# SwiGLU feed-forward on one core: the loads of the head issued in one line on SyncE's queue, the crossbar load of x rows 256 to 511 moved ahead of the first up weights, gate projection before up

## The chip, the cores and the metric

The kernel runs on one core of one Trainium2 chip. The metric is device time in microseconds (us) of that core. A profiled execution gives, besides, a span (first to last instruction) and a record of each instruction and each transfer; all start times below are counted from the start of that span.

## What is computed

The input x has 2048 rows of 640 numbers, the weights w_gate and w_up are 640 by 1536, and w_down is 1536 by 640, all bf16:

```python
def reference(x, w_gate, w_up, w_down):
    g = _silu(x @ w_gate)
    u = x @ w_up
    return (g * u) @ w_down
```

## The kernel before, in words

All three products run on TensorE. The 640 inner rows make 5 slices of 128 (KD, index kd), the 1536 hidden columns 12 slices (KF, index fc), and the 2048 rows of x four blocks of 512 (index sb). Gate and up are computed transposed: a weight slice of 128x128 is the stationary operand, and x transposed (xT, 128 partitions by kd by row) streams past it. So `proj` (line 193) makes five matmuls per output tile, one for each kd, and accumulates them in PSUM. `gate` (line 208) lets ScalarE take SiLU of the gate tile (L212) and VectorE multiply it with the up tile (L213) into aT. After the 12 slices of a block, the down projection multiplies aT with wd_sb (L270 and L299), and ScalarE copies and SyncE and ScalarE store the output. The last four rows of x are left to VectorE (`row_dots`, L148), which works them out beside TensorE.

**The head** is the first block's start, before all weights are there. x rows 0 to 255 come as two plain loads of 128 rows (x_sb, L86) and are transposed by TensorE (L186) and copied to xT by ScalarE and VectorE (L191). Rows 256 to 511 come by a transposing load through the DMA crossbar (`turn_x`, L110), straight into xT. Of the weights, the first chunk is 256 columns (fc 0 and 1), of gate and of up, 320 KB each; it is cut at kd = 2 (K_CUT) into a part of 128 KB and one of 192 KB.

In `head` (line 217) the order of TensorE's work is written out and fixed by `keep_order`: 18 filling matmuls on ones (L177), 10 transposes of x (L186), 2 more filling matmuls, then 14 matmuls of gate for fc 0 and 1 on x rows 0 to 255 (L237, the list `early`: kd 0 and 1 in halves of 128 columns, kd 2 to 4 in 256 columns). Then, in the kernel before, come up on rows 0 to 255 for fc 0 and 1 (10 matmuls of 256 columns), and then for each fc gate and up on rows 256 to 511 (20 matmuls of 256 columns). From fc = 2 on, every matmul of gate and up has 512 columns.

The loads are issued on two queues. SyncE (SPq) issues x rows 0 to 127, gate kd 0 to 1, up kd 2 to 4, the crossbar load, and after them the later weight chunks (L83), w_down (L126) and the rest. ScalarE (ACTq) issues x rows 128 to 255, gate kd 2 to 4 and up kd 0 to 1, then loads its SiLU table (L122). SyncE's issues keep their written order too (`keep_order` at the end). The four PSUM buffers with the tag `gu` hold the two gate and two up tiles of fc 0 and 1 at the same time.

Of the kernel before, what the change touches and what calls it, by code (L numbers as in the profile page):

```python
# [10 lines left out]
def _body(  # L11
# [8 lines left out]
    nc = tc.nc  # L20
# [12 lines left out]
    KD = D // P  # L33
    KF = F // P
    S_BLK = 512
# [8 lines left out]
    K_CUT = 2  # L44
    ROW_J = 0
    W_CHUNKS = [(0, 2), (2, 4), (4, 8), (8, 12)]
# [12 lines left out]
    wg_sb = consts.tile([P, KD, F], bf16)  # L59
    wu_sb = consts.tile([P, KD, F], bf16)  # L60
# [14 lines left out]
    wg_v = w_gate.rearrange("(kd p) f -> p kd f", p=P)  # L75
    wu_v = w_up.rearrange("(kd p) f -> p kd f", p=P)
    wd_v = w_down.rearrange("(kf p) d -> p kf d", p=P)

    def wslice(a, b):
        return slice(a * P, b * P)  # L80

    def load_w(eng, dst, src, a, b):
        eng.dma_start(out=dst[:, :, wslice(a, b)], in_=src[:, :, wslice(a, b)])  # L83

    def load_x(eng, c0, c1):
        eng.dma_start(out=x_sb[:, c0:c1, :], in_=x_v[:, c0:c1, :])  # L86
# [11 lines left out]
    def keep_order(engine):  # L98

        traced = [i for i in nc.cur_bb.bb.instructions if i.engine == engine]  # L100
        for a, b in zip(traced, traced[1:]):
            issue_order(a, b)
# [5 lines left out]
    def turn_x(c0, c1):  # L108
        s_sl = slice(c0 * P, c1 * P)
        nc.sync.dma_start_transpose(out=xT[:, :, s_sl], in_=xt_v[s_sl])  # L110

    load_x(nc.sync, 0, 1)
    load_x(nc.scalar, 1, 2)
    f_sl = wslice(*W_CHUNKS[0])
    for dst, src, first, second in (
        (wg_sb, wg_v, nc.sync, nc.scalar),
        (wu_sb, wu_v, nc.scalar, nc.sync),
    ):
        for eng, k_sl in ((first, slice(0, K_CUT)), (second, slice(K_CUT, KD))):
            eng.dma_start(out=dst[:, k_sl, f_sl], in_=src[:, k_sl, f_sl])  # L120
    turn_x(PE_X, SUB)
    nc.scalar.activation(silu_first[:], ones[:, 0:1], ACT.Silu)  # L122
    for a, b in W_CHUNKS[1:]:
        load_w(nc.sync, wg_sb, wg_v, a, b)
# [5 lines left out]
    def turn_w(dst, src):  # L130
# [7 lines left out]
        out=x_row[:],  # L138
        in_=x2[S - T : S, :].rearrange("t d -> (t d)").partition_broadcast(P),
# [35 lines left out]
    def warm(n):  # L175
        for _ in range(n):
            nc.tensor.matmul(  # L177
                pw[:, 0:P], lhsT=ones[:], rhs=ones[:], start=True, stop=True
            )

    def transpose_chunk(c, parts):
        c_sl = slice(c * P, (c + 1) * P)
        for copy, tag, k0, k1 in parts:
            pt = psum.tile([P, k1 - k0, P], bf16, tag=tag, name="pt")
            for kd in range(k0, k1):
                nc.tensor.transpose(  # L186
                    out=pt[:, kd - k0, :],
                    in_=x_sb[:, c, kd * P : (kd + 1) * P],
                    identity=ident[:],
                )  # L190
            copy(out=xT[:, k0:k1, c_sl], in_=pt[:])  # L191

    def proj(ps, w_sb, fc, sb, c0, c1):
        for kd in range(KD):
            nc.tensor.matmul(  # L195
                ps[:, c0:c1],
                lhsT=w_sb[:, kd, fc * P : (fc + 1) * P],
                rhs=xT[:, kd, sb * S_BLK + c0 : sb * S_BLK + c1],
                start=(kd == 0),
                stop=(kd == KD - 1),  # L200
            )

    def gu_tiles():
        pg = psum.tile([P, S_BLK], f32, tag="gu", name="pg", bufs=4)
        pu = psum.tile([P, S_BLK], f32, tag="gu", name="pu", bufs=4)
        return pg, pu

    def gate(pg, pu, sb, fc, n_s):

        s0 = sb * S_BLK  # L210
        sg = work.tile([P, S_BLK], f32, name="sg")
        nc.scalar.activation(sg[:, 0:n_s], pg[:, 0:n_s], ACT.Silu)  # L212
        nc.vector.tensor_tensor(  # L213
            out=aT[:, fc, s0 : s0 + n_s], in0=sg[:, 0:n_s], in1=pu[:, 0:n_s], op=ALU.mult
        )

    def head():

        dve, act = nc.vector.tensor_copy, nc.scalar.copy
        split = [(act, "po_a", 0, 2), (dve, "po_b", 2, KD)]
        late = PE_X * P
        (pg0, pu0), (pg1, pu1) = gu_tiles(), gu_tiles()
        warm(N_WARM)
        transpose_chunk(0, split)
        transpose_chunk(1, split)
        warm(N_GAP)  # L230
        early = [(kd, c * P, (c + 1) * P) for c in range(PE_X) for kd in range(K_CUT)]
        early += [(kd, 0, late) for kd in range(K_CUT, KD)]
        for kd, c0, c1 in early:
            for fc, pg in ((0, pg0), (1, pg1)):


                nc.tensor.matmul(  # L237
                    pg[:, c0:c1],
                    lhsT=wg_sb[:, kd, wslice(fc, fc + 1)],
                    rhs=xT[:, kd, c0:c1],  # L240
                    start=(kd == 0 and c0 == 0),
                    stop=(kd == KD - 1),
                )
        proj(pu0, wu_sb, 0, 0, 0, late)
        proj(pu1, wu_sb, 1, 0, 0, late)
        for fc, pg, pu in ((0, pg0, pu0), (1, pg1, pu1)):
            proj(pg, wg_sb, fc, 0, late, S_BLK)
            proj(pu, wu_sb, fc, 0, late, S_BLK)
            gate(pg, pu, 0, fc, S_BLK)
        keep_order(mybir.EngineType.PE)  # L250
        keep_order(mybir.EngineType.Activation)

    head()
    for sb in range(NSB):
        n_s = S_BLK if sb < NSB - 1 else S_BLK - T
        for fc in range(KF):
            if sb == 0 and fc < 2:
                continue
            pg, pu = gu_tiles()
# [22 lines left out]
        for q in range(P // Q):  # L282
            nc.scalar.dma_start(
                out=out2[
                    sb * S_BLK : sb * S_BLK + n_t, DA + q * Q : DA + (q + 1) * Q
                ].rearrange("(i r) c -> r i c", r=Q),
                in_=ot_q[q * Q : (q + 1) * Q, :].rearrange("r (i c) -> r i c", c=Q),
            )

        for j in range(SUB):  # L290
# [5 lines left out]
            for c0, c1, tag in cols:  # L296
# [10 lines left out]
                if c1 < D:  # L307
                    nc.scalar.copy(ot[:], po[:])  # L308
                    eng = nc.sync
                else:  # L310
                    nc.vector.tensor_copy(out=ot[:], in_=po[:])  # L311
                    eng = nc.scalar
# [81 lines left out]
def kernel(tc, *args):  # L394
    _body(tc, *args)
    tc.close()
    tc.compile()
    _trim(tc.nc)
# [30 lines left out]
```

## Time and profile before

| what | us |
|---|---|
| median of 3 runs (lowest, highest) | 163.66 (163.46, 163.86) |
| span of the profiled execution | 162.17 |
| median less span: what lies around the span, if that execution was a median one | 1.49 |
| TensorE busy, share of the span | 159.8, 99% |
| VectorE busy | 110.9 |
| ScalarE busy | 42.7 |
| first matmul of fc = 2 (the head's work is behind it) | 9.11 |

The profiled execution has no time of its own besides its span, so the median of the runs stands in for it. A matmul's record holds its whole passage through the array, and the next starts before it ends; so the pace is read from start to start. Of the span, 99% on the chain of waits that ended last is TensorE; the granted clock in the rows is full throughout. A transfer's row gives the queue that issued it, its size, and the time from issue to landing; issue start plus that time is when the waiting engine may go on.

### The profile page before, as it was taken

The numbers are of one execution on the slowest core, as the hardware profiler recorded it, in microseconds if no ns is written. First come the engines' busy times: TensorE is split into PE (matmuls) and PEld (weight loads), VectorE is DVE, ScalarE is ACT, GpSimd is POOL, SyncE is SP. The second block draws the span as 40 slices with busy tenths as digits, with TensorE's granted clock in tenths as the row PEclk, the third lists the DMA queues.
The fourth block names the chain that finished last, engine by engine and source line by source line (L and its number), as shares of the span: only waits on it lengthen the run. The fifth ranks groups of instructions, "written<-read, shape, count | busy, mean of one in ns | idle before, by whom it ended". The sixth has DMA issues, their size and how long they took to land.

```text
span 162.2 us, 2118 instructions
## 1 busy us (share of the span) xinstructions
PE 159.8 (99%) x798; PEld 77.9 (48%) x798; DVE 110.9 (68%) x249; ACT 42.7 (26%) x74; POOL 0.6 (0%) x6
## 2 busy tenths in 40 slices
PE   9999999999999999999999999999999999999995
PEld 8854444444444444444444444444444444445454
DVE  2042233599469999979919999979964999993000
ACT  5132222112222222221222322221214222222121
POOL 1000000000000000000000000000000000000000
PEclk9999999999999999999999999999999999999999
DMA  7999999994179992003110000000320000000312
GB/s 208 258 339 348 362 218 249 219 234 94 34 185 178 224 195 61 4 0 34 65 65 0 0 4 2 0 0 2 63 69 32 0 0 0 0 0 4 50 39 73
DMA packets 42441, 15.86 MB, mean 98 GB/s; under 512 B 33216, under 2 KB 42304, under 8 KB 42432
## 3 DMA queue, kind: packets, MB, share of 16 engines
q1 hardware_dynamic: 33536, 14.72, 37.7%
q10 hardware_dynamic: 8896, 1.02, 4.1%
q8 instruction: 6, 0.10, 0.2%
q14 instruction: 3, 0.02, 0.1%
HBM read 6.88 MB, written 2.62 MB: 59 GB/s over the span
## 4 chain that ended last, share of the span: by engine, by line
PE 99%; DVE 0%; issue 0%
PE pu L195 32%; PE pg L195 31%; PE po_a L299 26%; PE po_t L270 6%; PE pw L177 1%; PE pg L237 1%; PE pt L186 1%; DVE ot_b L311 0%; DVE ones L106 0%
## 5 line engine op out<-in xcount | busy, mean ns | idle before, releaser
L195 PE MATMUL pu<-xT,wu_sb 128*128 128x512 bf16 (+2 forms) x250 | 59.8, 370 | 0.0
L195 PE MATMUL pg<-xT,wg_sb 128*128 128x512 bf16 (+2 forms) x240 | 58.5, 374 | 0.0
L213 DVE TENSOR_TENSOR aT<-sg,pu 128x512 bf16<-128x512 f32 (+1 forms) x48 | 32.8, 683 | 32.8 <-PE pu L195 28.1
L212 ACT ACTIVATE sg<-pg 128x512 f32<-128x512 f32 (+1 forms) x48 | 28.6, 596 | 71.2 <-PE pg L195 68.1
L299 PE MATMUL po_a<-wd_sb,aT 128*128 128x512 bf16 (+2 forms) x216 | 42.8, 358 | 0.0
L148 DVE SCALAR_TENSOR_TENSOR prod<-wgT,x_row 128x640 f32<-128x640 bf16 x48 | 39.4, 821 | 1.1
L148 DVE SCALAR_TENSOR_TENSOR prod<-wuT,x_row 128x640 f32<-128x640 bf16 x48 | 39.4, 822 | 1.0
L195 PEld LDWEIGHTS <-wu_sb 128*128 128x128 bf16 x250 | 24.4, 98 | 27.6 <-DMA wu_sb<-in_w_up_dram 0.3
L195 PEld LDWEIGHTS <-wg_sb 128*128 128x128 bf16 x240 | 23.5, 98 | 26.9
L299 PEld LDWEIGHTS <-aT 128*128 128x128 bf16 x216 | 20.7, 98 | 21.6
L308 ACT CAST ot<-po_a 128x512 bf16<-128x512 f32 (+1 forms) x17 | 9.5, 560 | 32.0 <-PE po_a L299 20.8
L270 PE MATMUL po_t<-aT,wd_sb 128*128 128x512 bf16 (+1 forms) x48 | 10.4, 366 | 0.0
L270 PEld LDWEIGHTS <-wd_sb 128*128 128x128 bf16 x48 | 4.7, 98 | 5.1
L311 DVE CAST ot_b<-po_a 128x128 bf16<-128x128 f32 x1 | 0.3, 291 | 9.9 <-PE po_a L299 9.9
L279 ACT CAST ot_t<-po_t 128x512 bf16<-128x512 f32 (+1 forms) x4 | 2.2, 558 | 11.6 <-PE po_t L270 11.6
L148 DVE DVE_READ_ACCUMULATOR prod<-wuT,x_row 128x1 f32 x48 | 3.9, 82 | 0.0
L148 DVE DVE_READ_ACCUMULATOR prod<-wgT,x_row 128x1 f32 x48 | 3.9, 82 | 0.0
L281 DVE STREAM_TRANSPOSE ot_q<-ot_t 128x512 bf16<-128x512 bf16 (+1 forms) x4 | 2.7, 678 | 1.7 <-ACT ot_t L279 1.7
L177 PE MATMUL pw<-ones 128*128 128x128 bf16 x20 | 2.5, 313 | 0.4 <-DVE ones L106 0.4
L191 DVE COPY xT<-pt 128x384 bf16<-128x384 bf16 x2 | 0.7, 358 | 2.9 <-PE pt L186 2.9
L237 PE MATMUL pg<-xT,wg_sb 128*128 128x128 bf16 (+1 forms) x14 | 2.3, 360 | 0.0
L177 PEld LDWEIGHTS <-ones 128*128 128x128 bf16 x20 | 2.1, 148 | 0.4 <-DVE ones L106 0.4
(15 smaller groups left out, 7.6 us busy)
## 6 DMA issues: line engine op xcount, KB each, us to landing
wd_sb<-in_w_down_dram SPq DMA_DIRECT2D x1, 1920.0 KB, 14.5
out_dram<-ot SPq DMA_DIRECT2D x15, 128.0 KB, 1.7
wg_sb<-in_w_gate_dram SPq DMA_DIRECT2D x2, 640.0 KB, 7.7
wu_sb<-in_w_up_dram SPq DMA_DIRECT2D x2, 640.0 KB, 8.7
x_row<-in_x_dram SPq DMA_DIRECT2D x1, 640.0 KB, 4.7
out_dram<-ot_q ACTq DMA_DIRECT2D x12, 32.0 KB, 1.9
wg_sb<-in_w_gate_dram SPq DMA_DIRECT2D x1, 320.0 KB, 4.9
wu_sb<-in_w_up_dram SPq DMA_DIRECT2D x1, 320.0 KB, 5.4
```

Of the source, the lines that this page charges most:

```text
L148: nc.vector.scalar_tensor_tensor(out=prod[:], in0=wT[:, fc, :], scalar=1.0, in1=x_row[:, t, :], op0=ALU.mult, op1=ALU.mult, accum_out=acc[ ...
L177: nc.tensor.matmul(pw[:, 0:P], lhsT=ones[:], rhs=ones[:], start=True, stop=True)
L186: nc.tensor.transpose(out=pt[:, kd - k0, :], in_=x_sb[:, c, kd * P : (kd + 1) * P], identity=ident[:],)
L195: nc.tensor.matmul(ps[:, c0:c1], lhsT=w_sb[:, kd, fc * P : (fc + 1) * P], rhs=xT[:, kd, sb * S_BLK + c0 : sb * S_BLK + c1], start=(kd == 0 ...
L212: nc.scalar.activation(sg[:, 0:n_s], pg[:, 0:n_s], ACT.Silu)
L213: nc.vector.tensor_tensor(out=aT[:, fc, s0 : s0 + n_s], in0=sg[:, 0:n_s], in1=pu[:, 0:n_s], op=ALU.mult)
L237: nc.tensor.matmul(pg[:, c0:c1], lhsT=wg_sb[:, kd, wslice(fc, fc + 1)], rhs=xT[:, kd, c0:c1], start=(kd == 0 and c0 == 0), stop=(kd == KD ...
L270: nc.tensor.matmul(po_t[:], lhsT=wd_sb[:, kf, DA:D], rhs=aT[:, kf, sb * S_BLK : sb * S_BLK + n_t], start=(kf == 0), stop=(kf == KF - 1),)
L279: nc.scalar.copy(ot_t[:], po_t[:])
L281: nc.vector.transpose(out=ot_q[:], in_=ot_t[:])
L299: nc.tensor.matmul(po[:], lhsT=aT[:, kf, s0 : s0 + P], rhs=wd_sb[:, kf, c0:c1], start=(kf == 0), stop=(kf == KF - 1),)
L308: nc.scalar.copy(ot[:], po[:])
```

## The change

All six loads of the head (there were seven) are issued by SyncE, in the order x rows 0 to 127, x rows 128 to 255, gate kd 0 to 1, gate kd 2 to 4, the crossbar load of x rows 256 to 511, and then the first up chunk as one load of 320 KB. ScalarE issues none of them. On TensorE the 14 early gate matmuls stay; behind them now come gate on rows 256 to 511 for fc 0 and 1 (10 matmuls of 256 columns), and then for each fc up on all 512 rows (10 matmuls of 512 columns in all in place of 20 of 256).

```diff
     load_x(nc.sync, 0, 1)
-    load_x(nc.scalar, 1, 2)
+    load_x(nc.sync, 1, 2)
     f_sl = wslice(*W_CHUNKS[0])
-    for dst, src, first, second in (
-        (wg_sb, wg_v, nc.sync, nc.scalar),
-        (wu_sb, wu_v, nc.scalar, nc.sync),
-    ):
-        for eng, k_sl in ((first, slice(0, K_CUT)), (second, slice(K_CUT, KD))):
-            eng.dma_start(out=dst[:, k_sl, f_sl], in_=src[:, k_sl, f_sl])
+    for k_sl in (slice(0, K_CUT), slice(K_CUT, KD)):
+        nc.sync.dma_start(out=wg_sb[:, k_sl, f_sl], in_=wg_v[:, k_sl, f_sl])
     turn_x(PE_X, SUB)
+    load_w(nc.sync, wu_sb, wu_v, *W_CHUNKS[0])
     nc.scalar.activation(silu_first[:], ones[:, 0:1], ACT.Silu)
...
-        proj(pu0, wu_sb, 0, 0, 0, late)
-        proj(pu1, wu_sb, 1, 0, 0, late)
+        proj(pg0, wg_sb, 0, 0, late, S_BLK)
+        proj(pg1, wg_sb, 1, 0, late, S_BLK)
         for fc, pg, pu in ((0, pg0, pu0), (1, pg1, pu1)):
-            proj(pg, wg_sb, fc, 0, late, S_BLK)
-            proj(pu, wu_sb, fc, 0, late, S_BLK)
+            proj(pu, wu_sb, fc, 0, 0, S_BLK)
             gate(pg, pu, 0, fc, S_BLK)
```

## The prediction

> **What bounds the kernel now.** I read the page's busy times first (TensorE 159.8 of 162.2 us), then the chain of waits that ended last (99% TensorE, no transfer in it), then the timeline of the first 12 us, then the transfers. The change touches only the head, so its worth is the shift of one moment: the first matmul of fc = 2, at 9.11 in the timeline. From there on TensorE runs without a gap (five 512-column matmuls in 1.08 us, 9.11 to 10.19, again and again), so a shift of that moment should reach the end whole.
>
> The timeline's columns are start, length, engine and line. Start to start is the pace.
>
> ```profile
> 0.40 2.10 PE L177 MATMUL pw<-ones 128*128 128x128 bf16 x18 [0.40 <-DVE ones L106]
> ...
> 1.43 1.63 SPq L110 DMA_TRANSPOSE xT<-in_x_dram  x1
> ...
> 2.29 1.31 PE L186 MATMUL pt<-ident,x_sb 128*128 128x128 bf16 x10
> ...
> 3.61 2.34 PE L237 MATMUL pg<-xT,wg_sb 128*128 128x128 bf16 x14
> ...
> 5.80 1.01 PEld L195 LDWEIGHTS <-wu_sb 128*128 128x128 bf16 x10 [0.32 <-DMA wu_sb<-in_w_up_dram]
> 5.80 1.29 PE L195 MATMUL pu<-xT,wu_sb 128*128 128x256 bf16 x10
> ...
> 6.92 0.71 PE L195 MATMUL pg<-xT,wg_sb 128*128 128x256 bf16 x5
> ...
> 9.11 1.24 PE L195 MATMUL pg<-xT,wg_sb 128*128 128x512 bf16 x5
> ...
> 10.19 1.24 PE L195 MATMUL pu<-xT,wu_sb 128*128 128x512 bf16 x5
> ```
>
> See that TensorE is already back to back from 0.40: 18 filling matmuls take 1.89 us (0.105 each), and in the trace every 128-column matmul up to 4.36 starts 0.107 after the one before, and every 256-column one up to 5.53 takes 0.213. From 5.94 on a 256-column matmul takes 0.109 and a 512-column one 0.216. So TensorE runs at half pace until about 5.8, although the rows show the full granted clock, and the first 5.75 us of its work are bound by its own pace, not by a load. The only idle time is 0.05 us (5.75 to 5.80), where it waits for up weights.
>
> The head's transfers, from the list of transfers (last column: us from issue to landing):
>
> ```profile
> wg_sb<-in_w_gate_dram ACTq DMA_DIRECT2D x1, 192.0 KB, 3.6
> wu_sb<-in_w_up_dram SPq DMA_DIRECT2D x1, 192.0 KB, 4.7
> x_sb<-in_x_dram SPq DMA_DIRECT2D x1, 160.0 KB, 2.2
> x_sb<-in_x_dram ACTq DMA_DIRECT2D x1, 160.0 KB, 2.7
> wg_sb<-in_w_gate_dram SPq DMA_DIRECT2D x1, 128.0 KB, 2.8
> wu_sb<-in_w_up_dram ACTq DMA_DIRECT2D x1, 128.0 KB, 4.7
> ```
>
> The same list for issues between 1.4 and 3 us has the crossbar load:
>
> ```profile
> xT<-in_x_dram SPq DMA_TRANSPOSE x1, 5.4
> ```
>
> With the issue starts of the timeline the landings are: x rows 0 to 127 at 2.25, rows 128 to 255 at 2.85, gate kd 0 to 1 at 3.25, gate kd 2 to 4 at 4.20, up at 5.75, the crossbar load at 1.43 + 5.4 = 6.82. The head is balanced to within 0.1: up is there when gate is done (5.75), the crossbar load when up on 256 rows is done (6.9).
>
> **The change on TensorE.** Up to 5.75 nothing changes in work or order. After it, before: 30 matmuls of 256 columns, 30 x 0.109 = 3.27. After: 10 x 0.109 = 1.09 and 10 x 0.216 = 2.16, together 3.25. The change of pace costs 0.035 on one matmul either way (5.80 to 5.94). If no load is late, fc = 2 starts at 5.75 + 0.035 + 3.25 = 9.04 instead of 9.11: **-0.07 us**. ScalarE and VectorE: both SiLUs now start early, the first product (0.69) follows the first up tile at about 7.9, and the PSUM buffer that fc = 3 needs at about 11.2 is free near 7.7; nothing waits. ScalarE's table load, which began at 1.58 behind three issues of 0.41 to 0.51, starts sooner; the copy that it delayed is ahead of need anyway.
>
> **The change on the queue.** SP's issues take 0.40 to 0.47 and start 0.46 apart, so x rows 128 to 255 are issued at 0.46 (were at 0.12), gate at 0.92 and 1.38, the crossbar load at 1.85 (was 1.43) and, after its 1.63, up at 3.53. Needs and supplies:
>
> - x rows 128 to 255, needed at 2.83; before, landed at 2.85. Both x loads are ahead of all else now; the bytes that had moved by 2.2 were 320 KB, so about 2.6. Hidden.
> - Gate kd 2 to 4, needed at 4.36. Before, 640 KB had moved by 3.4, but shared with up; now the first 640 KB are just x and gate. Engines are up to 0.7 apart (completion packets of this load 3.14 to 3.84), so 3.8 for the last, plus 0.4 to land: 4.2. Bounds 3.9 and 4.5, price 0 to 0.15; I take 0.
> - The crossbar load, needed at 5.75 + 0.035. Three estimates. By bytes: 320 KB of up are no longer ahead of it; the next 320 KB load landed 1.16 behind it before (3.11 + 4.9 = 7.98), so 6.82 - 1.16 = 5.66. By issue: a crossbar load onto idle queues (issued at 44.88) had sent as many packets 2.75 after its issue; 1.85 + 2.75, plus 0.65 for landing as here, is 5.25. By the slowest engine, see below: 5.45. I take **5.45**, hidden by 0.3. Bounds: 5.25, and 1.85 + 5.4 = 7.25 if nothing is gained by going earlier.
> - Up, needed at 5.79 + 1.09 = 6.87. It stands behind the crossbar load as the later gate chunk did: 5.45 + 1.16 = **6.6**, hidden by 0.25. Bounds 6.4 and 8.4.
>
> The third estimate reads the transfer view from 4.5 to 5.5, 40 slices of 0.025 us:
>
> ```profile
> GB/s 338 246 297 348 287 246 297 246 277 225 236 236 225 195 164 195 164 164 102 143 123 92 51 92 31 0 20 20 20 10 20 20 20 143 174 154 205 123 133 174
> ```
>
> The rate falls to near nothing at 5.1 and comes back at 5.33. Crossbar packets of the fast engines hang there, and all are released together just after the slowest engine, done with up at 5.14, has begun its own. From its beginning to the end of all the packets it is 0.95 (5.1 to 6.05), then 0.7 to land. With the slowest engine done with gate at 3.8: 3.8 + 0.95 + 0.7 = 5.45.
>
> The later chunks keep their place: 1.28 MB lie ahead of them as before, and gate of fc 2 and 3 landed at 7.98 for a need at 9.11. If the covers above go, every us late at 5.79 or 6.87 is a us at the end.
>
> **Sum.** Span 162.17 - 0.07 = 162.10, plus the 1.49 around it, 163.59; I say **163.6** against the median of 163.66.
>
> **Rivals.**
>
> *The crossbar load stays the late one (slower).* The wait for up at 5.75 becomes one for xT, and up behind it is late too. For it: the load waits for the slowest of 16 engines, three loads of its kind further on show packets that hang 0.8 to 1.2, and it is issued 0.42 later. Against: 320 KB fewer ahead. It decides from a landing of 5.79 for xT or 6.87 for up. At 6.3, halfway to the upper bound from 5.45, fc = 2 starts at 6.3 + 3.25 = 9.55, and up (7.46 + 2.16 = 9.62) sets it: +0.5, **164.2**. At the upper bound it is 8.4 + 2.16 = 10.56, +1.45.
>
> *One queue starts its transfers a whole us apart (slower).* On SP's queue the first packets of its loads came at 1.02, 1.98, 3.05 and 4.10, while ScalarE's came between them. If that is one queue's own limit, gate kd 2 to 4 starts at 4, the crossbar load at 5.1, and lands 2.2 to 2.7 later, at 7.3 to 7.8; 3.25 more gives 10.6 to 11.0, **165.2 to 165.6**. Against it speak ScalarE's four stores at 112.5, alone on their queue, in slices of 0.06 us:
>
> ```profile
> GB/s 0 0 0 33 64 89 84 79 84 82 33 0 28 62 85 89 79 81 82 42 0 27 58 87 80 86 83 87 39 0 30 65 87 81 89 92 78 25 0 0
> ```
>
> They start 9 slices, 0.54 us, apart: one queue does one each half us, so the us in the head was two queues taking turns. [...]
>
> *The pace steps up earlier (faster).* In the one trace it steps at 5.8. If in other runs it steps at 4.3, the early gate ends at 4.36 + 6 x 0.109 = 5.0. Before, that gained nothing: up landed at 5.75, and 5.75 + 3.27 = 9.02. After, with the lower bounds (xT 5.25, up 6.4), fc = 2 starts at 6.4 + 2.16 = 8.56: -0.45, **163.2**. Against it: the spread of 163.46 to 163.86 gives no sign, and both loads must be at their best. [...]
>
> *The change doesn't do what it says.* The order on TensorE and SyncE is fixed by hand, so this would only mean that one load slips; it gives the forecast's time.
>
> **Chances.** Forecast 0.52 (with the last rival); crossbar load late 0.26; one queue a us apart 0.10; earlier step 0.12. A difference of 0.2%, 0.33 us, is about what a measurement of this kernel can tell from none. All of the first slower rival's and the second's chance counts as slower, so faster 0.12, same 0.52, slower 0.36. The range must leave out no more than 0.2: from 163.3 (part of the fast case) to 164.5 (most of the late crossbar load); the us-apart case lies beyond. The forecast's own range is 163.4 to 163.9.
>
> **What the profile of the changed kernel would show.** Right: 14 early gate matmuls ending near 5.75, gate of rows 256 to 511 at 5.8, up at 6.9, fc = 2 near 9.04; crossbar landing 3.6 after its issue at 1.85, up 3.1 after 3.53. Wrong: idle time of TensorE's weight loads put down to xT or wu_sb, first packets of SP's loads a us apart, x rows 128 to 255 landing past 2.85, or gate past 4.36, which would stretch the early gate.

## The result and the profile after

The changed kernel takes **164.87 us** (median of 4 runs, 164.81 to 165.12) beside 163.61 for the kernel before: ratio **1.0089**, 95% interval 1.0074 to 1.0105. A second measurement gave 164.78 beside 163.54 (1.0071, 1.0048 to 1.0095). The forecast was 163.6 with a range to 164.5; the change is slower. A ratio here is an estimate of its own from the same runs, not the quotient of the two medians beside it (1.0077 here), and for e3 it leaves out one slow run of 166.88, at a granted clock of 0.99.

The profiled execution has a span of 163.58 us, 1.41 more than before. The page's chain now has a transfer and SyncE's issues in it, where before it was TensorE alone:

```profile
PE 94%; DMA 3%; SPq 2%; issue 0%; DVE 0%
```

The timeline of the head (start, length, engine, line; in brackets idle time ahead and what ended it):

```profile
1.90 1.40 SPq L110 DMA_TRANSPOSE xT<-in_x_dram  x1
...
3.34 0.58 SPq L83 DMA_DIRECT2D wu_sb<-in_w_up_dram  x1
...
3.74 0.62 PE L234 MATMUL pg<-xT,wg_sb 128*128 128x128 bf16 x8
...
5.00 0.83 PE L234 MATMUL pg<-xT,wg_sb 128*128 128x256 bf16 x6 [0.64 <-DMA wg_sb<-in_w_gate_dram]
...
6.28 1.25 PE L192 MATMUL pg<-xT,wg_sb 128*128 128x256 bf16 x10 [0.45 <-DMA xT<-in_x_dram]
...
8.34 2.33 PE L192 MATMUL pu<-xT,wu_sb 128*128 128x512 bf16 x10 [0.81 <-DMA wu_sb<-in_w_up_dram]
...
10.51 1.24 PE L192 MATMUL pg<-xT,wg_sb 128*128 128x512 bf16 x5
```

See four starts of TensorE, each behind a load: gate kd 0 to 1 (3.74), gate kd 2 to 4 (5.00), the crossbar load (6.28), up (8.34). The gate of fc = 2 starts at 10.51 in place of 9.11, and these 1.40 us are the whole difference: span less start of fc = 2 is 153.07 us in the profiles of both kernels, and in all the experiments below to 0.01. So each run can be read by that one start.

The list of transfers of the changed kernel's head has the landings (last column: us from issue):

```profile
wu_sb<-in_w_up_dram SPq DMA_DIRECT2D x1, 320.0 KB, 4.9
...
wg_sb<-in_w_gate_dram SPq DMA_DIRECT2D x1, 192.0 KB, 3.6
wg_sb<-in_w_gate_dram SPq DMA_DIRECT2D x1, 128.0 KB, 2.8
xT<-in_x_dram SPq DMA_TRANSPOSE x1, 4.3
```

With the issue starts: gate kd 0 to 1 at 3.70, gate kd 2 to 4 at 4.96, the crossbar load at 6.24, up at 8.29.

A load's landing is the last of 16 completions, and the trace has each. Two things are seen there. First, gate kd 2 to 4: one completion at 3.79, then none for a whole us, then 15 from 4.79 to 4.96. The transfer view from 4 to 5 (slices of 0.025 us) shows why:

```profile
GB/s 256 256 266 287 276 307 287 297 297 184 184 154 102 82 61 41 20 20 20 20 20 21 20 20 10 20 20 20 20 92 205 225 143 287 297 276 276 307 287 287
```

From 4.25 the rate dies away to 20 GB/s, one packet of 512 bytes a slice, until 4.73: about what one engine moves alone, at 0.03 us a packet. Gate's completion packets (4 bytes each, 16 for this load) agree: 15 went by 3.91, the last at 4.55. Crossbar packets begun from 4.20 on hang, and end together between 4.73 and 4.77. I call the end of that stretch, 4.77, the **release**. Second, up: 15 completions from 7.26 to 7.36, and the last at 8.29. One engine is late by 0.93.

### The profile page after: what moved, and what is told of

It is laid out like the page before. It is cut to its first block, busy times and chain, and to the rows that moved or that the text cites. A ratio compares the mean times of both kernels' runs of the same rounds, so it can differ in the third digit from the quotient of the medians.

```text
span 163.6 us, 2097 instructions
## 1 busy us (share of the span) xinstructions
PE 159.2 (97%) x788; PEld 76.2 (47%) x788; DVE 110.9 (68%) x249; ACT 42.8 (26%) x74; POOL 0.6 (0%) x6
## 4 chain that ended last, share of the span: by engine, by line
PE 94%; DMA 3%; SPq 2%; issue 0%; DVE 0%
PE pu L192 32%; PE pg L192 30%; PE po_a L295 26%; PE po_t L266 6%; DMA wu_sb<-in_w_up_dram 3%; SPq L110 1%; SPq L116 1%; SPq L86 0%; DVE ot_b L307 0%
## 5 line engine op out<-in xcount | busy, mean ns | idle before, releaser
L192 PE MATMUL pu<-xT,wu_sb 128*128 128x512 bf16 (+1 forms) x240 | 59.4, 379 | 0.8 <-DMA wu_sb<-in_w_up_dram 0.8
L192 PEld LDWEIGHTS <-wu_sb 128*128 128x128 bf16 x240 | 23.4, 98 | 29.1 <-DMA wu_sb<-in_w_up_dram 1.1
L234 PE MATMUL pg<-xT,wg_sb 128*128 128x128 bf16 (+1 forms) x14 | 1.4, 243 | 0.8 <-DMA wg_sb<-in_w_gate_dram 0.6
```

Source lines behind the costliest of these rows:

```text
L192: nc.tensor.matmul(ps[:, c0:c1], lhsT=w_sb[:, kd, fc * P : (fc + 1) * P], rhs=xT[:, kd, sb * S_BLK + c0 : sb * S_BLK + c1], start=(kd == 0 ...
```

## The experiments

I started from theory A (the place of the crossbar load is the cost, by its release and by what stands behind it) and theory B (one queue in place of two is the cost).

### e1: one queue, up ahead of the crossbar load, TensorE's order as before

```diff
 (the kernel before)
     load_x(nc.sync, 0, 1)
-    load_x(nc.scalar, 1, 2)
+    load_x(nc.sync, 1, 2)
     f_sl = wslice(*W_CHUNKS[0])
-    for dst, src, first, second in (
-        (wg_sb, wg_v, nc.sync, nc.scalar),
-        (wu_sb, wu_v, nc.scalar, nc.sync),
-    ):
-        for eng, k_sl in ((first, slice(0, K_CUT)), (second, slice(K_CUT, KD))):
-            eng.dma_start(out=dst[:, k_sl, f_sl], in_=src[:, k_sl, f_sl])
+    for k_sl in (slice(0, K_CUT), slice(K_CUT, KD)):
+        nc.sync.dma_start(out=wg_sb[:, k_sl, f_sl], in_=wg_v[:, k_sl, f_sl])
+    load_w(nc.sync, wu_sb, wu_v, *W_CHUNKS[0])
     turn_x(PE_X, SUB)
```

> All loads on SyncE's queue as in the changed kernel, but the first up chunk ahead of the crossbar load, and TensorE's order as before. Theory A (the crossbar load's place is the cost: completions of the loads near it are held until its slowest engine has begun, and up stands behind it): gate kd 2 to 4 lands near 4.2, up near 5.7, the crossbar load near 6.8, fc = 2 starts near 9.1 to 9.3, time 163.6 to 163.8. Theory B (one queue in place of two is the cost: each load starts later): up lands past 7, fc = 2 past 10, time 164.5 or more.

Measured: 163.95 beside 163.40, ratio 1.0016 (1.0000 to 1.0031). Up landed at 5.90, the crossbar load at 7.07. Theory B's 164.5 is out; one queue by itself costs less than the whole change (the medians are 0.55 us apart, against 1.26 there). What it costs is seen in one row:

```profile
9.67 1.25 PE L192 MATMUL pg<-xT,wg_sb 128*128 128x512 bf16 x4 [0.22 <-DMA wg_sb<-in_w_gate_dram]
```

The gate chunk of fc 2 and 3, behind the crossbar load, has its median completion at 8.10 and its last at 9.63: again late engines in the load behind the crossbar load.

### e2: two queues, the crossbar load ahead of up, gate first

```diff
 (the changed kernel)
-    load_x(nc.sync, 1, 2)
+    load_x(nc.scalar, 1, 2)
-    for k_sl in (slice(0, K_CUT), slice(K_CUT, KD)):
-        nc.sync.dma_start(...)
+    for eng, k_sl in ((nc.sync, slice(0, K_CUT)), (nc.scalar, slice(K_CUT, KD))):
+        eng.dma_start(out=wg_sb[:, k_sl, f_sl], in_=wg_v[:, k_sl, f_sl])
```

> ScalarE issues x rows 128 to 255 and gate kd 2 to 4 again; on SyncE's queue x, gate kd 0 to 1, the crossbar load, then up; TensorE's order as in the changed kernel. Theory A: gate kd 0 to 1 is back at 3.25, but gate kd 2 to 4 still lands near 4.8, the crossbar load near 6.1 and up near 8.2; fc = 2 near 10.4, time 164.8. Theory B: gate kd 2 to 4 at 4.2, the crossbar load near 5.5, up near 6.6, time 163.6.

Measured: 164.43 beside 163.40, 1.0056 (1.0040 to 1.0072). The time is nearer to A's; the landings up to the crossbar load are nearer to B's (gate kd 2 to 4 at 4.34, the crossbar load at 5.49).

```profile
5.55 1.25 PE L192 MATMUL pg<-xT,wg_sb 128*128 128x256 bf16 x10
7.89 2.11 PE L192 MATMUL pu<-xT,wu_sb 128*128 128x512 bf16 x9 [1.09 <-DMA wu_sb<-in_w_up_dram]
9.84 1.24 PE L192 MATMUL pg<-xT,wg_sb 128*128 128x512 bf16 x5
```

Here the crossbar load did land at 5.49, where the forecast had put it (release 4.12), and gate on rows 256 to 511 followed the early gate without idle time. (The record of the first of the ten up matmuls, near 7.68, is missing.) It was no use: up came at 7.62 (median of its completions 6.96), where B had 6.6.

### e3: loads of the kernel before, gate first

```diff
 (the kernel before)
-        proj(pu0, wu_sb, 0, 0, 0, late)
-        proj(pu1, wu_sb, 1, 0, 0, late)
+        proj(pg0, wg_sb, 0, 0, late, S_BLK)
+        proj(pg1, wg_sb, 1, 0, late, S_BLK)
         for fc, pg, pu in ((0, pg0, pu0), (1, pg1, pu1)):
-            proj(pg, wg_sb, fc, 0, late, S_BLK)
-            proj(pu, wu_sb, fc, 0, late, S_BLK)
+            proj(pu, wu_sb, fc, 0, 0, S_BLK)
```

> TensorE's order of the changed kernel with the loads of the kernel before. The crossbar load should land at 6.8 and up at 5.75, so TensorE waits from the end of the early gate to 6.8 and then has 1.09 + 2.16 us of work: fc = 2 at 10.1, +0.95 on 9.11, time 164.6, by theory A and by theory B. If it is nearer to 163.6, the order on TensorE is no part of the cost.

Measured: 164.36 beside 163.40, 1.0046 (1.0025 to 1.0067); fc = 2 at 10.11, the expected 10.1. TensorE waits for xT:

```profile
6.87 1.25 PE L195 MATMUL pg<-xT,wg_sb 128*128 128x256 bf16 x10 [0.74 <-DMA xT<-in_x_dram]
8.17 2.10 PE L195 MATMUL pu<-xT,wu_sb 128*128 128x512 bf16 x9
10.11 1.24 PE L195 MATMUL pg<-xT,wg_sb 128*128 128x512 bf16 x5
```

Gate first makes x rows 256 to 511 the load that 3.25 us of work stand behind; with up first it is 2.2.

### e4: loads of the changed kernel, up first

```diff
 (the changed kernel)
-        proj(pg0, wg_sb, 0, 0, late, S_BLK)
-        proj(pg1, wg_sb, 1, 0, late, S_BLK)
+        proj(pu0, wu_sb, 0, 0, 0, late)
+        proj(pu1, wu_sb, 1, 0, 0, late)
         for fc, pg, pu in ((0, pg0, pu0), (1, pg1, pu1)):
-            proj(pu, wu_sb, fc, 0, 0, S_BLK)
+            proj(pg, wg_sb, fc, 0, late, S_BLK)
+            proj(pu, wu_sb, fc, 0, late, S_BLK)
```

> Loads of the changed kernel, TensorE's order of the kernel before: up on rows 0 to 255 ahead of gate on rows 256 to 511. If up lands at 8.3 as in the changed kernel, 30 matmuls of 0.109 follow it: fc = 2 at 11.6, time 166.0. If up lands at 7.3 (15 of its 16 completions came by 7.36 in the changed kernel, the last at 8.29), fc = 2 at 10.6, time 165.0.

Measured: 166.55 beside 163.40, 1.0174 (1.0122 to 1.0226).

```profile
8.13 1.27 PE L192 MATMUL pu<-xT,wu_sb 128*128 128x256 bf16 x10 [1.89 <-DMA wu_sb<-in_w_up_dram]
...
11.41 1.24 PE L192 MATMUL pg<-xT,wg_sb 128*128 128x512 bf16 x4
```

Up landed at 8.08 (median 6.77, four completions from 7.71 on), fc = 2 at 11.41, with 3.33 of work behind up. The profile is of an execution of 165.79. Two of the four took 165.8, at a granted clock of 1.00, and two 167.3, at 0.99; these two may have fallen back to half pace as e8 and e9 do below, but they have no profile. So each half of the change is slow without the other; together they lose less than this one and more than e3.

### e5: a plain load in the crossbar load's place

```diff
 (the changed kernel)
-    turn_x(PE_X, SUB)
+    nc.sync.dma_start(
+        out=xT[:, :, PE_X * P : SUB * P],
+        in_=x2[PE_X * P : SUB * P, :].rearrange("(p s) d -> p (s d)", p=P)
+            .rearrange("p (k c) -> p k c", k=KD))
```

> The changed kernel with a plain load of the same 320 KB (640 pieces of 512 bytes) in the place of the crossbar load, so that x rows 256 to 511 are not transposed: the transposition is left out. Theory A (the crossbar load holds the completions around it until its slowest engine has begun, and the load behind it has a late engine): gate kd 2 to 4 lands near 4.1 in place of 4.96, the plain load near 5.2, up near 6.3, all 16 completions of a load within 0.4; fc = 2 near 9.0, time 163.4 to 163.7. Theory B (one queue, and small loads on it): gate kd 2 to 4 still near 4.9, up still past 7.5, time 164.5 or more.

Measured: 164.05 beside 163.37, 1.0048 (1.0024 to 1.0071), between the two theories. The hold is gone: gate kd 2 to 4 completes from 3.92 to 4.50 without a gap. But

```profile
3.95 1.51 PE L237 MATMUL pg<-xT,wg_sb 128*128 128x128 bf16 x14 [0.18 <-DMA wg_sb<-in_w_gate_dram]
6.87 1.25 PE L195 MATMUL pg<-xT,wg_sb 128*128 128x256 bf16 x10 [1.41 <-DMA xT<-in_x_dram]
```

the plain load's median completion came at 5.29 and its last at 6.83; three engines were late. So half of theory A fell: late engines need no crossbar load ahead of them. Whether one makes them more frequent is not shown.

### e6: up issued by ScalarE

```diff
 (the changed kernel)
-    load_w(nc.sync, wu_sb, wu_v, *W_CHUNKS[0])
+    load_w(nc.scalar, wu_sb, wu_v, *W_CHUNKS[0])
```

> The changed kernel with the one load of the first up chunk issued by ScalarE, whose queue is otherwise empty: up no longer stands behind the crossbar load in a queue. Theory A: up is moved beside x and gate and lands near 5.7, held by the crossbar load until it is released; x and gate land 0.3 to 1 later, gate kd 2 to 4 with up near 5.2 to 5.7, and the crossbar load near 6.8, so fc = 2 starts near 6.8 + 3.25 = 10.1, time 164.4 to 164.6. Theory B: taking a load off the one queue gives back half of the loss, time about 164.2, with gate at 4.2.

Measured: 165.36 beside 163.37, 1.0111 (1.0079 to 1.0142). ScalarE's queue was empty, so up was issued at 0.12, ahead of x rows 128 to 255 (0.44). The list of transfers issued in the first us:

```profile
x_sb<-in_x_dram SPq DMA_DIRECT2D x2, 160.0 KB, 3.1
wu_sb<-in_w_up_dram ACTq DMA_DIRECT2D x1, 320.0 KB, 3.6
```

Up landed at 3.75, but x rows 128 to 255 at 4.23 (2.74 in the changed kernel), though they stand in another queue. These two loads went in the order of their issue, although in two queues: the packets of the second x load go from 2.8 on, when three quarters of up's are through. TensorE sat idle from 2.9 to 4.3 and kept its half pace to 9.0 (the ten 256-column matmuls of gate from 7.13 to 9.09 start about 0.20 apart), which both theories had left out.

### e7: the kernel before with a plain load in the crossbar load's place

The edit is that of e5, in the kernel before.

> The kernel before with a plain load of the same 320 KB in the place of the crossbar load: the transposition is left out. Theory A: up's completions are no longer held (before, its last packets went at 5.14 and its last completions came at 5.75): up lands near 5.2 to 5.4, the plain load near 6.2. TensorE is bound by its own pace to 5.75 where the clock steps up late, so the time gains 0 to 0.4: 163.0 to 163.4 beside the kernel before at 163.4. Theory B: no change, up at 5.75.

Measured: 163.52 beside 163.37, 1.0003 (0.9984 to 1.0022): no difference that can be told, as theory B said. Up landed at 5.63, the plain load at 6.54: without the crossbar load up's last completion came 0.12 ahead of the 5.75 before, and later than A's 5.2 to 5.4. So the crossbar load's hold costs the kernel before nothing that shows.

### e8: the next gate chunk ahead of the crossbar load

Theory C: the late engine comes from issuing a load while the crossbar load ahead of it is moving.

```diff
 (the changed kernel; this chunk leaves the loop behind)
+    load_w(nc.sync, wg_sb, wg_v, *W_CHUNKS[1])
     turn_x(PE_X, SUB)
     load_w(nc.sync, wu_sb, wu_v, *W_CHUNKS[0])
```

> The changed kernel with the next gate chunk (320 KB, fc 2 and 3) put ahead of the crossbar load, so that the up load behind it is issued (3.9 to 4.5) before the crossbar load's first packets go (about 4.7). Theory C (the late engine comes from issuing a load while the crossbar load in front of it is already moving): all 16 completions of up come within 0.2, up lands 1.2 behind the crossbar load, near 8.1 to 8.3, fc = 2 near 10.4, time 164.7. Rival: a late engine follows the crossbar load in one line whatever the issue times are, so that up's last completion is 2.0 behind it, near 9.0; fc = 2 near 11.2, time 165.5.

Measured: 166.26 beside 163.37, 1.0156 (1.0107 to 1.0204). The crossbar load's issue took 2.53 us, so up was issued at 5.0, when the crossbar packets had moved since 4.74: the order that C wanted to avoid. Yet up's 16 completions came within 0.11, 1.15 behind the crossbar load (8.58 after 7.43). C is out, and so is its rival's 9.0. (before_again, below, speaks against C too: the load behind the crossbar load was issued by 3.73, ahead of the first crossbar packet at 4.12, and had a late engine all the same.) The time was worse than either theory said, by the pace:

```profile
5.24 0.83 PE L236 MATMUL pg<-xT,wg_sb 128*128 128x256 bf16 x6 [0.70 <-DMA wg_sb<-in_w_gate_dram]
7.47 2.29 PE L194 MATMUL pg<-xT,wg_sb 128*128 128x256 bf16 x10 [1.41 <-DMA xT<-in_x_dram]
9.56 2.94 PE L194 MATMUL pu<-xT,wu_sb 128*128 128x512 bf16 x10
12.34 1.24 PE L194 MATMUL pg<-xT,wg_sb 128*128 128x512 bf16 x5
```

The ten matmuls from 7.47 start 0.208 apart, where the six from 5.24 were 0.111 apart: after 0.9 and 1.6 us of idle time TensorE is back at half pace. The view by stretches says the same: its granted clock is 1.00 from 4.0 to 7.3, 0.50 from 7.5 to 10.7 and 1.00 again from 11 on.

### e9: two queues, up behind gate on ScalarE's

```diff
 (e2)
-    load_w(nc.sync, wu_sb, wu_v, *W_CHUNKS[0])
+    load_w(nc.scalar, wu_sb, wu_v, *W_CHUNKS[0])
```

> As e2 (two queues, crossbar load third on SyncE's queue, gate first on TensorE), but ScalarE issues the first up chunk, behind gate kd 2 to 4: up does not stand behind the crossbar load in a queue. Theory A (loads move in the order of issue whichever queue, and what follows the crossbar load in one queue lands 1.2 behind it or later): up, issued at 1.0 right after the crossbar load, shares the engines with it; the crossbar load's release comes when the slowest engine gets to it, and both land between 6.3 and 7.0; fc = 2 near 6.6 + 3.25 = 9.9, time 164.1 to 164.4, so no better than e2 by more than 0.4. Theory B (the place behind the crossbar load in the queue is the whole cost): crossbar load at 5.5 as in e2, up near 6.0, fc = 2 near 9.0, time 163.4.

Measured: 168.08 beside 163.83, 1.0252 (1.0213 to 1.0291): the slowest of all, and both theories missed it.

```profile
9.04 2.29 PE L192 MATMUL pg<-xT,wg_sb 128*128 128x256 bf16 x10 [3.04 <-DMA xT<-in_x_dram]
11.12 2.68 PE L192 MATMUL pu<-xT,wu_sb 128*128 128x512 bf16 x10
```

The crossbar load, issued at 0.91, landed at 8.99, 8.1 later; up, on the other queue beside it, at 8.79. Their packets went side by side, crossbar packets from 3.22 to 7.12, and in this profile both landed later than in either order in one queue (e1: 5.90 and 7.07; the changed kernel: 6.24 and 8.29). About 1.3 us of the time are not the loads' but the pace's: TensorE is idle from 5.8 to 9.0, its granted clock is 0.50 from 8.5 to 11.8, and the work behind xT takes 4.6 us (9.04 to 13.64) in place of 3.3. Without that it would still be the slowest of all.

### More profiles of both kernels

> The changed kernel once more, one look. If the late engine of up's load (last completion 0.93 behind the fifteenth) belongs to this line of loads, up's last completion again comes 0.7 to 1.2 behind the median; if it was chance (single packets of 0.2 to 0.8 us that fall on one engine), the lag is anywhere between 0.1 and 1.2 and the start of fc = 2 moves with it, between 9.6 and 10.6. The crossbar load's landing should again be 1.4 to 1.5 behind its release, and gate kd 2 to 4 within 0.3 behind that release.

> As after_again_1: a third look at the same kernel, for the spread of the release, of up's last completion and of the step of TensorE's pace.

> The kernel before once more, one look. If its head is bound by TensorE's pace and by loads that are all there in time, fc = 2 starts at 9.0 to 9.2 again, whether the pace steps up at 3 or at 6; a late engine in the gate chunk behind the crossbar load (needed at 9.1, landed at 7.98) up to 1.1 costs nothing.

Measured: 163.97 and 165.03 for the changed kernel, 163.14 for the kernel before. The first profiled execution of the changed kernel above took 164.89, a fourth (below) 165.16. Starts in after_again_1, then in before_again:

```profile
6.04 1.25 PE L192 MATMUL pg<-xT,wg_sb 128*128 128x256 bf16 x10 [0.42 <-DMA xT<-in_x_dram]
7.42 2.33 PE L192 MATMUL pu<-xT,wu_sb 128*128 128x512 bf16 x10
9.59 1.24 PE L192 MATMUL pg<-xT,wg_sb 128*128 128x512 bf16 x5
```

```profile
3.67 1.29 PE L237 MATMUL pg<-xT,wg_sb 128*128 128x128 bf16 x14
5.42 1.26 PE L195 MATMUL pu<-xT,wu_sb 128*128 128x256 bf16 x10 [0.47 <-DMA wu_sb<-in_w_up_dram]
...
8.76 1.24 PE L195 MATMUL pg<-xT,wg_sb 128*128 128x512 bf16 x5
```

In after_again_1 the last engine was only 0.27 behind the median and fc = 2 started at 9.59; this is the changed kernel without the late engine, and it is still 0.5 behind 9.11. before_again did not keep to 9.0 to 9.2: its pace stepped up at about 3.6, it then waited for up, which landed at 5.37, and fc = 2 started at 8.76. In that execution the load behind the crossbar load had its last completion 0.72 behind the median, at 8.30, with no wait for it.

### e10 and a control: does the late engine come from what is read?

```diff
 (the changed kernel)
-    load_w(nc.sync, wu_sb, wu_v, *W_CHUNKS[0])
+    load_w(nc.sync, wu_sb, wg_v, *W_CHUNKS[0])
```

> The changed kernel with the first up chunk read from the gate chunk's place in HBM, which the head has read 1.5 us earlier: up of fc 0 and 1 is computed with gate's weights. Theory D (the late engine comes from slow packets at the first read of a place in HBM): up's last completion within 0.3 of the median, in all runs; fc = 2 at 9.3 to 9.6, time 163.7 to 164.0, a spread of 0.4. Rival (a late engine does not depend on what is read): as the changed kernel beside it, 164 to 165.1 from run to run.

> The changed kernel beside e10 on the same chip, timed: 164 to 165.1, median near 164.8; the lag of up's last completion 0.2 to 1.4.

Measured: e10 164.89, the control 164.78, beside 163.54: 1.0081 (1.0051 to 1.0112) and 1.0071 (1.0048 to 1.0095), no difference. Up's last completion came 1.17 behind the median in e10 and 1.13 in the control. Theory D is out.

### The completions side by side

From the trace's completion and packet records, in us from the span's start, for every profile with a crossbar load in its head, but for e9. "Held" is the last completion of the load just ahead of the crossbar load, "behind" the load just behind it.

| kernel | release | held, last | crossbar load, last | less release | behind: median | last | fc = 2 |
|---|---|---|---|---|---|---|---|
| before | 5.36 | 5.75 (up) | 6.82 | 1.46 | 7.92 (gate, fc 2 and 3) | 7.98 | 9.11 |
| after | 4.77 | 4.96 | 6.24 | 1.46 | 7.31 (up) | 8.29 | 10.51 |
| after_again_1 | 4.55 | 4.75 | 5.99 | 1.44 | 7.10 (up) | 7.37 | 9.59 |
| after_again_2 | 4.44 | 4.62 | 5.86 | 1.42 | 6.92 (up) | 8.44 | 10.65 |
| after_timed_again | 4.94 | 5.09 | 6.37 | 1.43 | 7.43 (up) | 8.56 | 10.77 |
| before_again | 5.07 | 5.37 (up) | 6.53 | 1.46 | 7.58 (gate, fc 2 and 3) | 8.30 | 8.76 |
| e1 | 5.74 | 5.90 (up) | 7.07 | 1.33 | 8.10 (gate, fc 2 and 3) | 9.63 | 9.67 |
| e2 | 4.12 | 4.34 | 5.49 | 1.38 | 6.96 (up) | 7.62 | 9.84 |
| e3 | 5.41 | 5.73 (up) | 6.83 | 1.42 | 7.93 (gate, fc 2 and 3) | 7.98 | 10.11 |
| e4 | 4.43 | 4.61 | 5.84 | 1.41 | 6.77 (up) | 8.08 | 11.41 |
| e6 | 5.13 | 5.29 | 6.39 | 1.26 | 7.44 (gate, fc 2 and 3) | 7.87 | 11.25 |
| e8 | 6.01 | 6.17 (gate, fc 2 and 3) | 7.43 | 1.42 | 8.53 (up) | 8.58 | 12.34 |
| e10 | 4.86 | 5.04 | 6.32 | 1.46 | 7.32 (up) | 8.50 | 10.71 |

e9 does not fit the table: there the hung packets end in several groups between 4.14 and 5.16, and the crossbar load lands 3.8 behind the last of them.

## Why the prediction was wrong

**Right: TensorE's work.** fc = 2 = up's landing + 0.05 + 2.17 in after, after_again_1 and e2, and xT's landing + 3.3 in e3 and e5 (6.83 to 10.11 and 10.12). The 3.25 us of the working stand, and so does the working's step that a shift of fc = 2 reaches the end whole (153.07 us from there to the end of the span, to 0.01 in every profile).

**Right in kind: the release.** The third estimate said that all engines wait for the slowest, and that the landing follows a fixed time later. In the table it does, 1.26 to 1.46 behind the release; and the release comes 0.21 to 0.46 after the last completion packet of the loads ahead of the crossbar load, that is, after the slowest engine is done with them. after_timed_again is the exception: seven hung packets end by 4.54, 0.21 after that packet, the rest only at 4.94, and why is not known. (The working took the crossbar packets of the kernel before to end at 6.05. That holds for 1217 of 1280; the last end at 6.29, inside the 0.7 allowed for landing.)

**Wrong: "With the slowest engine done with gate at 3.8".** This step took the spread of the engines from the kernel before, where gate had been issued at 0.46 and 0.57. In the changed kernel the packets of the slowest engine's gate end at 4.55 (4.22 to 4.33 in the three other profiles), the release is at 4.44 to 4.94 in place of about 4.05, and the crossbar load lands at 5.86 to 6.37 in place of 5.45. Gate kd 2 to 4 itself, given bounds of 3.9 and 4.5, landed at 4.62 to 5.09. Much of it is the one queue: gate kd 0 to 1 is issued 0.45 later and lands at 3.70 in place of 3.25, and in e2, with two queues, the last of gate's completion packets went at 3.79, the release was at 4.12 and the crossbar load landed at 5.49. That is one profile of e2, so the share is not exact.

**Wrong: "Up stands behind the crossbar load as the later gate chunk did: 5.45 + 1.16".** The 1.16 is about right for the median engine (1.06 to 1.11 in the four profiles), and wrong for the last, which sets the landing: 1.38 to 2.58. The row it was taken from, 7.98 in the kernel before, happened to have all 16 completions within 0.09; in before_again they lay 0.75 apart, in e1 1.6. I took one record of one load for a property of loads.

**The sum, with what was measured**, in the first profile: crossbar load late 0.79 (6.24 for 5.45), up's late engine 0.93 (8.29 for 7.36), the fifteenth engine 0.04 earlier than 1.16 would have it, 0.04 for the start, less the 0.25 of cover: 1.47, and fc = 2 came at 10.51 in place of 9.04. So both covers, 0.3 and 0.25 us, were thinner than the scatter of what they covered.

**Why the kernel before does not pay.** Its crossbar load lands later, at 6.82, and the same lateness falls on the load behind it (7.98). But only 2.2 us of work of the head stand behind xT there, not 3.25, and the load behind it is not needed until 9.1, 1.1 after it landed. The change put up, with the tightest need, into that place. e3 (gate first alone, +0.46%) and e4 (the loads alone, +1.74%) show that neither half brings the gain, and e1 (+0.16%, 0.55 us by the medians) that the one queue by itself is the smaller part.

**The rivals.** "The crossbar load stays the late one" is the one that came: the waits named there, for xT and then for up, are those of the timeline; 164.2 was too low since up's late engine was not in it. "A whole us apart" did not come: x rows 128 to 255, second in the one queue, landed at 2.74, within their need. The condition of "the pace steps up earlier" did come: in the first profile of the changed kernel the pace stepped up at about 3.3 and the early gate had time to spare, but waited for its loads. The step moved from one profile to the next: it came at 3.3, 3.6 and 5.9 in after, before_again and before. The granted clock of 1.00 in the rows ahead of the step (0.00 to 3.20 in after) shows nothing: the clock's record in the trace begins with the step, at 5.89 in before and 3.27 in after, and in the rows a stretch without a record counts as full. And my remark that an early step gained the kernel before nothing does not hold in general: before_again, with the step at 3.6 and up landed at 5.37 in place of 5.75, had fc = 2 0.35 earlier.

**The hold** itself, which was not in the working, costs nothing by itself here: gate kd 2 to 4 at 4.96 let the early gate end at 5.67, ahead of xT at 6.24. In the kernel before it is seen across the two queues: up's part on ScalarE's queue, whose last packets went by 4.70 on 15 of 16 engines, completed only from 5.39 on, just behind the release at 5.36 of the crossbar load on SyncE's. In the changed kernel the held completions (4.79 to 4.96, release at 4.77) stand ahead of the crossbar load in its own queue. What holds them is not shown.

**Open:** why one to eight engines fall 0.3 to 1.5 us behind in some profiles and none in others. It needs no crossbar load ahead (e5), and it is neither issuing beside one (e8) nor a first read (e10), as far as one profile each can tell. The first profiles of the two kernels show single packets of 0.2 to 0.5 us where 0.03 is usual (0.46 and 0.48 at 2.61 and 2.65 in the changed kernel), mostly near the start of a load; whether these are the cause, and whether one queue makes them worse, is not settled: the lag of the load behind was 0.06, 0.06 and 0.72 with the loads of the kernel before, and 0.05 to 1.5 in one queue. A version that beats the kernel before did not come out of these runs.

## What to carry to other kernels

When a load is moved behind another, its landing has to be estimated for the last of the 16 engines, over several profiled executions, and the cover has to be larger than that scatter; here a cover of 0.3 us, taken from one execution, was none. The transposing load here let its hung packets go only 0.21 to 0.46 us behind the slowest engine's last packet of the loads ahead (12 of 13 profiles), and what stood behind it landed 1.15 to 2.6 us after it, so put behind such a load what is needed last, not next. When an order of work is swapped, write down for each load how much work stands behind it: the load that is slowest to land should have the least.

## What the hardware showed that was not expected

- A crossbar load's packets hang until the slowest engine is done with the loads ahead (release 0.21 to 0.46 after that engine's last packet in 12 of 13 profiles), and the load lands 1.26 to 1.46 behind that release. Completions of the load ahead are held as well, by about 0.8 us in the first profile of the changed kernel: the first came 0.33 behind its packet, those of packets from 3.67 to 3.91 only at 4.79 to 4.96.
- It puts the engines in step: its own completions come within 0.21 of each other in every profile of the table, and a lag gathered behind it stays, 0.98, 1.00 and 0.99 in up and the two loads after it in the first profile of the changed kernel.
- Loads of two queues can go in the order of issue: a load issued 0.33 us behind one of 320 KB on the other queue landed 1.5 later than without it (e6). Two issued 0.12 apart went side by side (the two parts of up in the kernel before, and e9).
- A crossbar load and a plain load side by side on two queues took 8.1 and 7.8 us to land (e9, one profile), against 4.6 and 4.3 one behind the other (e2).
- TensorE fell back to half pace after idle stretches of 0.9 and 1.6 us (e8) and after one of 3.2 (e9), but not in the changed kernel with 0.8, 0.6 and 1.0, nor in after_again_2 with 0.3, 0.6 and 1.5. In the clock's record of e8 and of e9 a full stretch of 3.41 us (3.98 to 7.39 in e8) is followed by a half one of 3.41. In e8 TensorE was busy for 1.4 us of that full stretch. What makes the pace fall back is not shown.
